# Joining attention and its output projection: the last head's last tiles transposed on TensorE, the first transposed load in two parts, the weight loads apart

## The chip, the cores and the metric

One core of a Trainium2 chip. The metric is the device time of one launch in microseconds (us). The engines are TensorE (PE, with its weight loads PEld), VectorE (DVE), ScalarE (ACT), GpSimd (POOL) and SyncE (SP), whose queue issues nearly all DMAs here. L559 is line 559 of the kernel before.

## The reference

A transformer block whose two halves are modulated by a condition c. D is 640, there are 2048 rows, 32 heads of 128, and 2048 cached keys and values for each head. Everything comes as bf16.

```python
mod = silu(c) @ w_mod                       # six rows: sa, ca, ga, sb, cb, gb
h = layernorm(x) * (1 + ca) + sa
q = (h @ wq) in 32 heads                    # wq: 640 x 4096
p = softmax(q @ k_cache^T / sqrt(128))      # 2048 x 2048 for each head
x = x + ga * ((p @ v_cache) @ wo)           # wo: 4096 x 640
h = layernorm(x) * (1 + cb) + sb
g = gelu(layernorm(h) @ w1)                 # w1: 640 x 640
hs = (four column groups of g shifted by +1, -1, +2, -2 rows) @ w2
x1 = h + hs
x = x + gb * (x1 + gelu(layernorm(x1) @ w3) @ w4)   # w3: 640 x 1728, w4: 1728 x 640
```

## The kernel before

**Planning.** `Prog` records every operation with the keys that it reads and writes, derives the semaphore waits from these, and emits the operations of each engine in the order in which they were recorded. So an engine's order is the order of the Python code, and a key that two operations share is a wait. SP's queue is such an order too: a DMA that waits holds those recorded after it.

**Score loop.** A tile is 128 rows of one head; there are NG = 512 tiles, 16 for each head, and step s of the loop begins tile s. PE multiplies queries and keys into `Sps` (L286), DVE scales with a minimum (L559, two halves), POOL joins the two minima (L569), ACT takes the exponential into `Pb`, one of eight rows of `ring` (L572). The probabilities have to be transposed for the product with the values: most tiles go in pairs through a DMA transpose on SP (`transpose`, L222), tiles 3 and 10 of each head through PE (`t_piece`, L253, into the banks `Oaug` and `QPp`), from which ACT (L262) or DVE (L264) copies them. `pv` (L299) multiplies with the values, 8 to 11 steps after the tile began; ACT copies each pair of results (L550), and POOL divides by the sums (`rcp` L440, `norm` L447) and writes four tiles at a time to `o_scratch` in DRAM (L454). Four tiles are a group, gr; head 31 has groups 124 to 127. The loop runs on past the last tile to step 523, for the products of the last eight tiles and their normalization.

**Output projection.** `load_ot(pr)` (L495) reads 256 rows of all 32 heads transposed from `o_scratch`: 64 blocks of 128x128, into `hTx` for even pr and into the place of `negS` for odd pr. It waits for the writes of all heads (`osd` keys). `load_xt` (L500) reads x again, in four parts, into rows of `ring` that tiles used before. The first `load_ot`, the four `load_xt` and the second `load_ot` follow each other on SP at step 512 and 513. Then i runs over 16 row tiles: `a_pe` (L631) multiplies with `wo`, 32 matmuls of 512 columns and 32 of 128, into one of two banks; `a_s1` and `a_s2` on DVE add, take statistics (L619, L621, with POOL's L612 and L614) and modulate; `nrm_of` (L662) writes a normed tile to one of three buffers, and `n_t` (L668) transposes it by DMA on SP. Statistics and the constant `mhalf` (L609) lie in the space of `On`, the buffer from which L454 writes.

**Second half.** `b_op` (L720; ACT evaluates gelu, L728) multiplies with w1, `c_op` (L740, DVE L744) with w2, `d_op` (L756, L760) with w3 and `e_op` (L772) with w4. The ten `b_op` of the first two column blocks come after the output projection; then each `c_op` is followed by one or two operations of a list of fillers, first `b_op`, then `d_op` and `e_op`. w3 and w4 go into the place of `wo` after the last product with it (L688, L689, L691), and all three loads write the one key `"wo"`.

Of the kernel before, what the change touches and what calls it, by code (L numbers as in the profile page):

```python
# [115 lines left out]
def bass_adaLN_cond__mha_block_cached__mixer_s_mlp__prompt_kernel(  # L116
# [6 lines left out]
    KT = D // 128  # L123
# [14 lines left out]
    with ExitStack() as es:  # L138
# [11 lines left out]
        if True:  # L150
            with ExitStack() as es1:
# [49 lines left out]
                G = Prog(nc, es1, "a")  # L201

                def load_k(h):
                    hb = h % 2
                    G.dma("sync", lambda e: e.dma_start_transpose(KTs[:, hb], A_k_cache[0, h]), ("k", hb), w=[("KT", hb)])
# [11 lines left out]
                assert RPB % 2 == 0 and RPT % 2 == 0 and NQT % 2 == 0  # L217
                is_pe = lambda g: g % NQT in PE_TILES

# [45 lines left out]

                by_dve = lambda g, r: r == 1 and g % NQT == PE_TILES[0]

# [64 lines left out]
                if H > 1:  # L332
                    load_wq(1)
                    load_k(1)
                G.dma("sync", lambda e: e.dma_start(wo[:], A_wo.rearrange("(h p) n -> p h n", p=128)), "wo", w=["wo"])

# [157 lines left out]
                def load_ot(pr):  # L494
                    G.dma("sync", lambda e: e.dma_start_transpose(OTj[pr % 2], o_scr[pr].rearrange("q h z d -> q (h z d)")),  # L495
                          ("ot", pr % 2), r=[("osd", pr // 2, hh) for hh in range(H)],
                          w=[("OT", pr % 2)] + ((HTK if pr == 0 else NEG) if pr < 2 else []))

# [7 lines left out]
                PVS, at = {}, []  # L506
                for g in range(NG):
# [5 lines left out]
                for g in range(NG):  # L513
                    NORMS.setdefault(at[g] + LAG, []).append(g)
                OT0 = max(NG, at[NG - NQT + 3] + LAG + 1)
                for s in range(at[-1] + LAG + 1):
                    h, j = divmod(s, NQT)
# [9 lines left out]
                    for half in range(2):  # L527
                        if s < NG:
                            qk(s, half)
                        for g_ in pvs:  # L530
                            if len(pvs) == 1:
                                pv(g_, half)
                            elif g_ == pvs[half]:
                                pv(g_, 0)
                                pv(g_, 1)
                        if s == 0 and half == 1:
                            q_head0(NQC - 1)
                        if h + 1 < H and 2 * j + half in QPIECE:
# [4 lines left out]
                        for r in range(2):  # L543
                            g = s - 3 - r
                            if 0 <= g < NG and is_pe(g):
                                t_piece(g, r, half)
                                if half == 1:
                                    evacs.append((t_evac, g, r))
                    for p in [g_ // 2 for g_ in pvs if g_ % 2 == 1]:
                        G.op("scalar", lambda a, p=p: a.copy(  # L550
                            Of[:, p % 4].rearrange("p z d -> p (z d)")[:, 0:259], PO[:, (p % 2) * 512:(p % 2) * 512 + 259]),
                            r=[("O", p % 2)], w=[("Of", p % 4)])
                    for fn, x, y in evacs:
# [14 lines left out]
                    if s < NG:  # L568
# [17 lines left out]
                    for g_ in NORMS.get(s, []):  # L586
# [11 lines left out]
                YB = [Sps[:, 0:1024], Sps[:, 1024:2048]]  # L598
                NB = [PTp[:, 0:1024], PTp[:, 1024:2048]]
# [3 lines left out]
                def ybank():  # L603
                    yn[0] += 1
                    return yn[0] % 2

                G.dma("sync", lambda e: e.dma_start(w1, B_w1.rearrange("(k p) n -> p k n", p=128)), "w1", w=["w1"] + KVK)
                G.dma("sync", lambda e: e.dma_start(w2, B_w2.rearrange("(k p) n -> p k n", p=128)), "w2", w=["w2"] + NEG)
                G.op("gpsimd", lambda g: g.memset(mhalf, -0.5), w=["mhalf"] + ONK)  # L609

# [12 lines left out]

                def a_pe(j):
                    b = ybank()
                    pr, z = divmod(j, 2)

                    def f(t):
                        for c0, cw in NC2:
                            for hh in range(H):  # L630
                                ins = t.matmul(YB[b][:, c0:c0 + cw], OTj[pr % 2][:, 2 * hh + z, :], wo[:, hh, c0:c0 + cw],  # L631
                                               start=(hh == 0), stop=(hh == H - 1))
                        return ins
                    G.op("tensor", f, r=[("OT", pr % 2), "wo"], w=[("S", b)])
                    return b

# [33 lines left out]

                for i in range(NQT + 1):
                    if i < NQT:
                        b = a_pe(i)
                        if i == NQT - 3:
                            for z in range(2):
                                G.op("gpsimd", lambda g, z=z: g.memset(us[:, :, z * SQ:z * SQ + 4], 0.0), w=[("usz", z), ("OT", 0)])  # L676
                        if i % 2 == 1 and (i + 3) // 2 < NQT // 2:
                            load_ot((i + 3) // 2)
                        a_s1(i, b)
                    if 1 <= i:  # L680
                        a_s2(i - 1)
                    if 2 <= i:
                        nrm_of(1, i - 2)
                        n_t(i - 2, i == 2)
                nrm_of(1, NQT - 1)
                n_t(NQT - 1, False)
                w3s = B_w3.rearrange("(k p) n -> p k n", p=128)
# [3 lines left out]
                G.dma("sync", lambda e: e.dma_start(w4[0:FL, NFT - 1, :], B_w4[(NFT - 1) * 128:FF, :]), "w4b", w=["w4b", "wo"])  # L691
                DEL = [1, -1, 2, -2]
# [22 lines left out]
                def b_op(cc, n):  # L715
# [14 lines left out]
                    G.op("scalar", ev, r=[("J", jb), ("usz", 0), ("usz", 1)], w=[("us", cc, n), ("OT", 0)])  # L730

                def c_op(j):
                    b = ybank()
# [29 lines left out]
                def e_op(j):  # L763
# [11 lines left out]
                    if j == NQT - 1:  # L775
                        for c0, cw in NC2:
                            G.op("tensor", lambda t, c0=c0, cw=cw: f(t, [(c0, cw)]), r=["w4", "w4b", ("gT", g)],
                                 w=[("S", b)] if c0 == 0 else [("S2", b)])
# [8 lines left out]
                        return  # L787
                    G.op("tensor", f, r=["w4", "w4b", ("gT", g)], w=[("S", b)])
                    G.op("vector", lambda v: v.tensor_add(out=tmp[:, u], in0=YB[b][:, 0:D], in1=xb[:, j]),  # L789
# [3 lines left out]
                    G.op("vector", lambda v: v.tensor_add(out=ob[:, u], in0=tmp[:, u], in1=xt[:, j]),  # L793
                         r=[("tmp", u), ("x1", j)], w=[("ob", u)] + (["wo"] if j < 2 else []))
# [56 lines left out]
```

## Time and profile before

| | us |
|---|---|
| runs shown: median of 3 (lowest, highest) | 1612.44 (1609.82, 1612.7) |
| the profiled execution | 1616.39 |
| its span | 1614.6 |
| PE busy in the span | 1483.7 (92%) |
| DVE busy | 1395.0 (86%) |
| ACT busy | 1268.3 (79%) |

The span is the time from the first to the last instruction that the profile holds; the execution's own time is 1.8 us longer. Matmuls overlap, so that PE counts as busy also where it is not at its peak. The core's mean granted TensorE clock is 0.993 of full speed. The chain of waits is followed back from the last instruction to what released each step; in the timeline, a bracket at a line's end tells how long the engine was idle before it and what ended that. "SPq" rows are the SP queue's own issue of a DMA, not the transfer.

### The profile page before, as it was taken

To read this page: it belongs to the slowest core of one execution; us is meant where nothing else is said; L and a number is where in the kernel's file an instruction comes from. 1 tells how busy PE (TensorE), PEld (TensorE's weight loads), DVE (VectorE), ACT (ScalarE), POOL (GpSimd) and SP (SyncE) were. 2 spreads that over 40 slices of the span, in tenths; PEclk is the share of its full clock that TensorE was granted. 3 is DMA by queue.
4 is the path that set the end of the run, shared out by engine and by line. 5 is a ranking of instruction groups with operands and counts; after the bars stand their busy time and mean duration, and the time that the engine had idled before them with its cause. 6 is when DMAs were issued, how large, how long until landed. Compare 5 with 4: busy or idle time off the path is not lost.

```text
span 1614.6 us, 34520 instructions
## 1 busy us (share of the span) xinstructions
PE 1483.7 (92%) x13820; PEld 954.8 (59%) x14071; DVE 1395.0 (86%) x2461; ACT 1268.3 (79%) x1113; POOL 627.2 (39%) x1396
## 2 busy tenths in 40 slices
PE   4799999999999999999999999998999699999999
PEld 3466666666666666666666666666666555544444
DVE  6999999999999999999999999998999446766424
ACT  4999999999999999999999999999999500033230
POOL 0144444444444444444444444444444513332100
PEclk9999999999999999999999999999999899999999
DMA  9999999999999999999999999999999998723100
GB/s 297 237 226 242 235 239 227 239 229 247 233 235 230 237 231 231 248 237 241 239 237 228 239 233 242 233 236 235 241 234 236 255 208 161 128 80 101 37 17 33
DMA packets 1189234, 338.85 MB, mean 210 GB/s; under 512 B 1169809, under 2 KB 1183057, under 8 KB 1189073
## 3 DMA queue, kind: packets, MB, share of 16 engines
q1 hardware_dynamic: 1182928, 319.83, 102.1%
q0 software_dynamic: 6144, 16.79, 3.1%
q8 instruction: 111, 1.82, 0.5%
q14 instruction: 51, 0.41, 0.1%
HBM read 43.48 MB, written 19.40 MB: 39 GB/s over the span
## 4 chain that ended last, share of the span: by engine, by line
DVE 25%; DMA 24%; ACT 23%; PE 18%; issue 9%; POOL 1%; SPq 0%; ACTq 0%; DVEq 0%; POOLq 0%
DVE negS L559 22%; DMA ring<-ring 21%; ACT ring L572 19%; PE Sps L631 7%; PE Sps L772 4%; PE Oaug L756 2%; PE QPp L756 2%; ACT ring L262 1%; ACT Of L550 1%; DMA wo<-in_B_w_dram 1%; ACT kv L244 1%; DMA ring<-in_A_x_dram 1%; DMA negS<-o_scratch 1%; DVE ring L364 1%; PE Sps L286 1%
## 5 line engine op out<-in xcount | busy, mean ns | idle before, releaser
L559 DVE TENSOR_SCALAR_CACHE_REDUCE negS<-Sps 128x1024 f32<-128x1024 f32 x1024 | 1180.1, 1225 | 38.8 <-ACT ring L572 18.8
L572 ACT ACTIVATE ring<-negS,small 128x2048 bf16<-128x2048 f32 x512 | 1007.7, 2017 | 39.6 <-DMA ring<-ring 33.7
L299 PEld LDWEIGHTS PTp<-kv,ring 128*128 128x128 bf16 x8192 | 560.1, 98 | 245.8 <-DMA ring<-ring 8.8
L286 PE MATMUL Sps<-kv 128*128 128x512 bf16 x1949 | 595.8, 383 | 76.1 <-DVE negS L559 54.9
L299 PE MATMUL PTp<-kv,ring 128*128 128x129 bf16 x8192 | 646.0, 221 | 6.9 <-DMA ring<-ring 6.8
L569 POOL TENSOR_SCALAR small<-small 128x1 f32<-128x1 f32 x512 | 146.5, 286 | 638.1 <-DVE negS L559 638.0
L286 PEld LDWEIGHTS Sps<-kv 128*128 128x128 bf16 x2048 | 126.8, 97 | 197.5 <-DVE negS L559 161.4
L447 POOL TENSOR_SCALAR On<-Of,small 128x128 bf16<-128x128 f32 x512 | 191.0, 374 | 13.0
L440 POOL TENSOR_TENSOR small<-Of,small 128x4 f32<-128x4 f32 x128 | 133.2, 1040 | 8.5 <-ACT Of L550 8.4
L454 POOL DMA_DIRECT2D o_scratch<-On x128 | 103.1, 806 | 40.8 <-POOL On L447 37.2
L237 PE MATMUL Oaug<-hTx,kv 128*128 128x512 bf16 x265 | 100.8, 385 | 12.7 <-ACT ring L262 7.7
L550 ACT COPY Of<-PTp 128x259 f32<-128x259 f32 x256 | 96.9, 379 | 11.0 <-PE PTp L299 11.0
L728 ACT ACT_TABLE_LOAD x1 | 1.3, 1283 | 129.8 <-POOL hTx L676 129.8
L237 PE MATMUL QPp<-hTx,kv 128*128 128x512 bf16 x259 | 96.7, 378 | 3.4 <-ACT hTx L391 2.7
L559 DVE DVE_READ_ACCUMULATOR negS<-Sps 128x1 f32 x1024 | 90.8, 89 | 0.0
L612 POOL TENSOR_SCALAR On<-On 128x1 f32<-128x1 f32 x48 | 24.3, 507 | 146.0 <-DVE On L621 146.0
L639 DVE TENSOR_TENSOR ring<-Sps,mod_bc 128x640 f32<-128x640 f32 x16 | 13.2, 825 | 74.1 <-PE Sps L631 74.1
L631 PE MATMUL Sps<-wo,hTx 128*128 128x128 bf16 (+1 forms) x504 | 71.1, 303 | 4.8 <-DMA hTx<-o_scratch 4.4
L631 PE MATMUL Sps<-wo,negS 128*128 128x128 bf16 (+1 forms) x504 | 69.1, 298 | 2.2 <-DMA negS<-o_scratch 1.8
L789 DVE TENSOR_TENSOR ring<-Sps,ring 128x640 f32<-128x640 f32 x15 | 12.4, 825 | 65.5 <-PE Sps L772 65.5
L262 ACT COPY ring<-Oaug 128x1024 bf16<-128x1024 bf16 x64 | 65.5, 1023 | 0.0
L631 PEld LDWEIGHTS Sps<-wo,hTx 128*128 128x128 bf16 x512 | 40.0, 99 | 36.1 <-DMA hTx<-o_scratch 4.3
(83 smaller groups left out, 986.7 us busy)
## 6 DMA issues: line engine op xcount, KB each, us to landing
kv<-in_A_v_cache_dram SPq DMA_DIRECT2D x32, 512.0 KB, 5.0
o_scratch<-On POOLq DMA_DIRECT2D x128, 128.0 KB, 5.4
ring<-in_A_x_dram SPq DMA_DIRECT2D x8, 640.0 KB, 4.9
kv<-in_A_wq_dram SPq DMA_DIRECT2D x32, 160.0 KB, 3.9
wo<-in_A_wo_dram SPq DMA_DIRECT2D x1, 5120.0 KB, 16.7
ring<-ring SPq DMA_TRANSPOSE x256, 7.2
ring<-in_w_mod_dram SPq DMA_DIRECT2D x1, 3200.0 KB, 14.2
out_dram<-wo SPq DMA_DIRECT2D x16, 160.0 KB, 1.8
```

The lines of the kernel that those rows point to most:

```text
L237: G.op("tensor", lambda t: t.matmul(JB[jb], wq[:, hb, q, :], hT[:, q, cc * 512:(cc + 1) * 512], start=(q == 0), stop=(q == KT - 1)), r=[(" ...
L262: G.op("scalar", lambda a: a.copy(dst, src), r=[("J", jb)], w=[("PT", g % RPT, r)])
L286: ins = t.matmul(Sps[:, col:col + 512], QT[:, hb, j * 128:(j + 1) * 128], KTs[:, hb, col:col + 512], start=True, stop=True)
L299: ins = t.matmul(ob[:, 0:129], PTs[:, b, kt, :], Vaug[:, hb, kt, 0:129], start=(kt == 0), stop=(kt == NKT - 1))
L440: G.op("gpsimd", lambda g: g.tensor_tensor(out=rl[:, 4 * b:4 * b + 4], in0=Of[:].rearrange("p a z d -> p (a z) d")[:, 4 * b:4 * b + 4, 128 ...
L447: G.op("gpsimd", lambda g: g.tensor_scalar(out=On[:, b, z, :], in0=Of[:, 2 * b + z // 2, z % 2, 0:128], scalar1=rl[:, 4 * b + z:4 * b + z ...
L454: G.dma("gpsimd", lambda e: e.dma_start(o_scr[jj // 2:jj // 2 + 2, :, hh].rearrange("a p z d -> p a (z d)"), On[:, b].rearrange("p (a z) d ...
L550: G.op("scalar", lambda a, p=p: a.copy(Of[:, p % 4].rearrange("p z d -> p (z d)")[:, 0:259], PO[:, (p % 2) * 512:(p % 2) * 512 + 259]), r= ...
L559: G.op("vector", lambda v, half=half, s=s, r8=r8: v.tensor_scalar(out=negS[:, s % 3, half * 1024:(half + 1) * 1024], in0=Sps[:, half * 102 ...
L569: G.op("gpsimd", lambda g, r8=r8: g.tensor_scalar(out=nm[:, r8:r8 + 1], in0=nm0[:, r8:r8 + 1], scalar1=nm1[:, r8:r8 + 1], scalar2=None, op ...
L572: G.op("scalar", lambda a, s=s, r8=r8: a.activation(Pb[:, s % RPB, :], negS[:, s % 3, :], ACT.Exp, bias=nm[:, r8:r8 + 1], scale=-1.0), r=[ ...
L631: ins = t.matmul(YB[b][:, c0:c0 + cw], OTj[pr % 2][:, 2 * hh + z, :], wo[:, hh, c0:c0 + cw], start=(hh == 0), stop=(hh == H - 1))
```

## The change

The last four tiles (508 to 511) are transposed by PE, with copies by DVE (five) and ACT (three); tile 506 now goes by DMA together with 507. The loop ends at step 511, and the value products of the last eight tiles are written out after it. The first `load_ot` is cut: 31 heads at step 504, head 31 (2 blocks) after the loop. Products 0 and 1 with `wo` are cut into pieces (`a_part`) that stand between the transposes and the value products. Group 124 is normalized at step 508 (before: at 510 and 511), group 126 last. The x loads and the second `load_ot` change their order, and w1 and w2 are recorded after the value products. The `b_op` of the first column block come before and after the last product with `wo`. The key `"wo"` becomes five keys, so that w3, w4 in two parts, and the rest of w4 each have their own; the w4 loads move behind `c_op` 4, 6 and 7. The core of the diff:

```diff
+                LAST_PE = NG - 4
+                LAST_DVE = ((LAST_PE, 0), (LAST_PE, 1), (LAST_PE + 1, 0), (LAST_PE + 1, 1), (LAST_PE + 3, 0))
+                is_pe = lambda g: g >= LAST_PE or (g % NQT in PE_TILES and (g < NG - NQT or g % NQT == PE_TILES[0]))
...
+                def load_ot0(h0, h1):
+                    G.dma("sync", lambda e: e.dma_start_transpose(
+                        OTj[0][:, 2 * h0:2 * h1, :], o_scr[0, :, h0:h1].rearrange("q h z d -> q (h z d)")),
+                        ("ot0", h0), r=[("osd", 0, hh) for hh in range(h0, h1)],
+                        w=[("OT", 0)] + HTK if h0 == 0 else [("OTB", 0)])
...
-                for s in range(at[-1] + LAG + 1):
+                for s in range(NG):
...
+                        if s == NG - 8:
+                            load_ot0(0, H - 1)
...
-                    if s == OT0:
-                        load_ot(0)
-                        for cc in range(NQC):
-                            load_xt(cc)
-                    if s == OT0 + 1:
-                        load_ot(1)
...
+                def a_part(j, h0, h1, parts):
+                    b = (j + 1) % 2
...
+                    G.op("tensor", f, r=[("OTB", 0) if pr == 0 and h0 == H - 1 else ("OT", pr % 2)] + WOK, w=[("S", b)])
...
+                def t_all(g, r):
+                    for q in range(2):
+                        t_piece(g, r, q)
+                    t_evac(g, r)
+                def pv2(g):
+                    for g_ in (g, g + 1):
+                        for half in range(2):
+                            pv(g_, half)
+                    of_copy(g // 2)
+                for g in (NG - 4, NG - 3):
+                    for r in range(2):
+                        t_all(g, r)
+                norm4(H * 4 - 3)
+                load_ot0(H - 1, H)
+                a_part(0, 0, H // 2, NC2[0:1])
+                for r in range(2):
+                    t_all(NG - 2, r)
+                a_part(0, H // 2, H - 1, NC2[0:1])
+                for r in range(2):
+                    t_all(NG - 1, r)
+                pv2(NG - 4)
+                a_part(0, 0, H - 1, NC2[1:2])
+                pv2(NG - 2)
+                norm4(H * 4 - 1)
+                load_xt(0)
+                load_ot(1)
+                for cc in range(1, NQC):
+                    load_xt(cc)
+                a_part(1, 0, H - 1, NC2)
+                for j in range(2):
+                    a_part(j, H - 1, H, NC2)
+                pv2(NG - 8)
+                pv2(NG - 6)
+                norm4(H * 4 - 2)
...
+                FIRST_B = {NQT - 2: (0, 1), NQT - 1: tuple(range(2, KT))}
...
                 for i in range(NQT + 1):
                     if i < NQT:
                         b = a_pe(i)
...
+                        for n in FIRST_B.get(i, ()):
+                            b_op(0, n)
                         a_s1(i, b)
...
-                G.dma("sync", lambda e: e.dma_start(w3, w3s), "w3", w=["w3", "wo"])
-                G.dma("sync", lambda e: e.dma_start(w4[:, 0:NFT - 1, :], B_w4[0:(NFT - 1) * 128, :].rearrange("(f p) n -> p f n", p=128)),
-                      "w4", w=["w4", "wo"])
-                G.dma("sync", lambda e: e.dma_start(w4[0:FL, NFT - 1, :], B_w4[(NFT - 1) * 128:FF, :]), "w4b", w=["w4b", "wo"])
+                G.dma("sync", lambda e: e.dma_start(w3, w3s), "w3", w=["w3", ("wo", 0)])
...
+                    if j in (4, 6, 7):
+                        load_w4((4, 6, 7).index(j))
...
-                for cc in range(2):
-                    for n in range(KT):
-                        b_op(cc, n)
+                for n in range(KT):
+                    b_op(1, n)
```

`norm4(gr)` is `rcp(gr)` and four `norm(gr, z)`. Products 0 and 1 in `a_pe` only name their bank now.

More of the change, by code (lines that the diff above doesn't have):

```diff
@@ L201, in bass_adaLN_cond__mha_block_cached__mixer_s_mlp__prompt_kernel @@
                 G = Prog(nc, es1, "a")
+                WOK = [("wo", i) for i in range(5)]
                 def load_k(h):
@@ L264, in t_evac @@
                         G.op("vector", lambda v: v.tensor_copy(dst, src), r=[("J", jb)], w=[("PT", g % RPT, r)])
-                by_dve = lambda g, r: r == 1 and g % NQT == PE_TILES[0]
+                by_dve = lambda g, r: (g, r) in LAST_DVE if g >= LAST_PE else r == 1 and g % NQT == PE_TILES[0]
+                TPIECE = {}
+                for g in range(LAST_PE):
+                    if is_pe(g):
+                        for r in range(2):
+                            TPIECE.setdefault(g + 3 + r, []).append((g, r))
                 taken = [u for j in PE_TILES for u in range(2 * (j + 3), 2 * (j + 5))]
@@ L512, in bass_adaLN_cond__mha_block_cached__mixer_s_mlp__prompt_kernel, with of_copy, norm4 @@
                 NORMS = {}
[L513 to L516 removed]
+                for g in range(NG - 12):
+                    gr = g // 4
+                    NORMS.setdefault(at[NG - NQT + 3] + 1 if gr == H * 4 - 4 else
+                                     max(at[gr * 4 + 3], at[g] + 2) if gr == H * 4 - 5 else at[g] + LAG, []).append(g)
+                assert at[-1] == NG - 1 and max(NORMS) < NG
+                def of_copy(p):
+                    G.op("scalar", lambda a: a.copy(
+                        Of[:, p % 4].rearrange("p z d -> p (z d)")[:, 0:259], PO[:, (p % 2) * 512:(p % 2) * 512 + 259]),
+                        r=[("O", p % 2)], w=[("Of", p % 4)])
+                def norm4(gr):
+                    rcp(gr)
+                    for z in range(4):
+                        norm(gr, z)
+                for s in range(NG):
                     h, j = divmod(s, NQT)
@@ L542, in bass_adaLN_cond__mha_block_cached__mixer_s_mlp__prompt_kernel @@
                                 evacs.append((q_evac, h + 1, cc))
[L543 to L548, printed above, removed]
+                        for g, r in TPIECE.get(s, []):
+                            t_piece(g, r, half)
+                            if half == 1:
+                                evacs.append((t_evac, g, r))
                     for p in [g_ // 2 for g_ in pvs if g_ % 2 == 1]:
-                        G.op("scalar", lambda a, p=p: a.copy(
-                            Of[:, p % 4].rearrange("p z d -> p (z d)")[:, 0:259], PO[:, (p % 2) * 512:(p % 2) * 512 + 259]),
-                            r=[("O", p % 2)], w=[("Of", p % 4)])
+                        of_copy(p)
                     for fn, x, y in evacs:
@@ new lines, in bass_adaLN_cond__mha_block_cached__mixer_s_mlp__prompt_kernel @@
+                G.dma("sync", lambda e: e.dma_start(w2, B_w2.rearrange("(k p) n -> p k n", p=128)), "w2", w=["w2"] + NEG)
+                G.op("gpsimd", lambda g: g.memset(mhalf, -0.5), w=["mhalf"] + ONK)
+                for i in range(NQT + 1):
+                    if i < NQT:
+                        b = a_pe(i)
+                        if i == NQT - 3:
+                            for z in range(2):
+                                G.op("gpsimd", lambda g, z=z: g.memset(us[:, :, z * SQ:z * SQ + 4], 0.0), w=[("usz", z), ("OT", 0)])
+                        if i % 2 == 1 and (i + 3) // 2 < NQT // 2:
+                            load_ot((i + 3) // 2)
+                        for n in FIRST_B.get(i, ()):
+                            b_op(0, n)
+                        a_s1(i, b)
+                    if 1 <= i:
+                        a_s2(i - 1)
+                    if 2 <= i:
+                        nrm_of(1, i - 2)
+                        n_t(i - 2, i == 2)
```

60 lines of the change are left out of this document (26 added, 34 removed).

## The prediction

> **What bounds the kernel now.** I read the busy time by stage first, with the stage limits taken from the chain of waits in order of time; then that chain; then the timeline of PE, POOL and the SP queue at the two seams that the change touches. Columns of the first view: start and end, length, then busy time and instructions of PE, PEld, DVE, ACT, POOL, then granted clock, DMA share, GB/s.
>
> ```profile
> 1270.00:1290.00 20.00, 9.40 (x125) 8.73 (x124) 0.01 (x1) 4.98 (x7) 11.54 (x22) 0.76 1.24 253
> 1290.00:1311.10 21.10, 19.27 (x126) 10.32 (x128) 4.42 (x8) 0.00 (x0) 0.85 (x3) 0.90 0.94 226
> 1311.10:1432.80 121.70, 120.97 (x882) 68.79 (x896) 81.25 (x151) 1.28 (x1) 40.52 (x58) 1.00 0.70 135
> 1432.80:1470.10 37.30, 31.69 (x166) 14.64 (x168) 24.51 (x48) 21.38 (x36) 9.88 (x18) 1.00 0.52 150
> 1470.10:1614.60 144.50, 139.54 (x803) 67.55 (x818) 62.85 (x100) 33.42 (x56) 12.90 (x22) 1.00 0.12 33
> ```
>
> The score loop ends near 1270. From 1311.1 to 1432.8 and from 1470.1 to the end PE is full, so what reaches those stretches earlier ends earlier by as much. Open time lies in the first two rows and in the fourth. The chain shows who holds them (start, length, what; lines are L numbers of the kernel):
>
> ```profile
> 1278.77 7.28 DMA o_scratch<-On
> 1286.05 1.33 SPq L495
> 1287.42 4.40 DMA ring<-in_A_x_dram
> ...
> 1298.02 12.84 DMA negS<-o_scratch
> 1310.86 0.27 issue
> 1311.13 8.64 PE Sps L631 x63
> ...
> 1454.39 8.48 DMA wo<-in_B_w_dram
> 1462.89 0.56 SPq L691
> 1463.49 2.78 DMA kv<-Of
> ```
>
> Until 1311 one SP queue leads: transposed loads and x loads one behind the other, then the second outputs' load (12.84). At 1454 to 1463 the w4 load stands ahead of the small transposes of the normed tiles. The timeline at those places:
>
> ```profile
> 1257.28 4.69 SPq L222 DMA_TRANSPOSE ring<-ring  x1
> 1262.02 4.26 SPq L222 DMA_TRANSPOSE ring<-ring  x1
> 1269.59 4.23 PE L299 MATMUL PTp<-kv,ring 128*128 128x129 bf16 x64 [0.74 <-DMA ring<-ring]
> 1275.66 2.04 PE L299 MATMUL PTp<-kv,ring 128*128 128x129 bf16 x32 [1.85 <-DMA ring<-ring]
> 1281.88 3.65 PE L299 MATMUL PTp<-kv,ring 128*128 128x129 bf16 x32 [4.17 <-DMA ring<-ring]
> 1288.87 0.78 POOL L454 DMA_DIRECT2D o_scratch<-On  x1 [0.29 <-POOL On L447]
> 1289.97 19.35 PE L631 MATMUL Sps<-wo,hTx 128*128 128x512 bf16 x126 [4.45 <-DMA hTx<-o_scratch]
> 1292.28 0.10 POOL L609 MEMSET On<- 128x1 f32 x1 [2.63 <-DMA o_scratch<-On]
> 1466.38 0.61 DVE L662 TENSOR_SCALAR Of<-ring,On 128x640 bf16<-128x640 f32 x1 [5.01 <-DMA kv<-Of]
> ```
>
> PE waits 1.85, 4.17 and 4.45 us for DMA transposes. After 1.85 us of idleness 32 value products took 2.04; after 4.17 they took 3.65, and the first wo product took 10.7 (1289.97 to the DVE's start at 1300.66) against 8.69 for each later one: the clock of 0.76 in the first table.
>
> **Part by part. 1. Outputs of 31 heads loaded early.** The load (62 blocks of 128x128) stands in SP's queue behind the transpose that starts at 1257.28, hence where the next pair starts now, 1262.02: the queue runs back to back here. Full loads of 64 blocks landed 11.5 to 14.9 us after issue, median 11.8 (line 495), and 62 blocks at the median give 11.4: PE may start its products at 1273.4 (1273.1 to 1276.5). Behind it come the pairs 504/505 and 506/507. A load holds the queue 8.0 (alone) to 11.6; I take 9.3 between busy neighbours, then 4.3 for each pair: issued at 1271.3 and 1275.6, landed 7.4 later, 1278.7 and 1283.0. The value products of these four tiles are put last on PE, so this delay lies under PE's other work. The x load must wait for the second pair (it overwrites its source), so it goes at 1283; the second outputs' load follows at 1283.7 and lands 12.84 later, at 1296.5. If all SP transposes cost 0.18 a block (11.56/64, the slowest row), it lands at about 1302.
>
> **2. What PE does from 1269.** Tiles 508 and 509 are transposed by PE with DVE copies of 0.69 (line 264), four of them after DVE's last minimum at 1270.0: done by about 1273, beside the wait for the load. POOL now normalizes group 124 at step 508 instead of 510/511: 1.04 + 1.42 + 0.8 ahead of the next minimum (L569), which may delay the exponentials of 509 to 511 by up to 2.6. Two ACT copies of 1.01 for tile 506 are gone at the same place, and PE wants tile 510 at 1277 only, so I cost it nothing; if that cover were gone it would be those 2.6. Then, in PE's order, from 1273.4: two wo products, 2 x 8.69 = 17.4; transposes of 510 and 511, 32 in eights (four take 0.39, so 8 take 0.44 to 0.78; I take 0.65) = 2.6; eight value products of 16, twice the 64 in 4.23 = 8.5. Together 28.5, with some joints of 0.05, 28.8: third product at 1302.2, not 1311.1. **Gain 8.9.** Value products at 0.94 each (as in the loop) and the shortest transposes would give 10.7.
>
> **3. The last normalization moves behind all that.** Group 126 is now the last written from buffer On, whose space the DVE statistics and the L609 memset take over; they wait until this write has landed. Now it is 6.75 from the end of the value products (1285.53) to the memset (1292.28), with a landing of 3.4. The changed one ends its products at 1302.1 amid w1, w2 and the third outputs' load, so I take the median landing 5.2 to 5.4: free at 1310.7. DVE has read product 0, but stands in its statistics; only after 0.9 + 0.2 + 0.84 does it free the bank of product 1, at 1312.6, where PE wants it at 1310.9. **Loss 1.6**; with landings of 3.3 to 7.3 (line 454), 0 to 3.8. DVE has 6.0 of work per 8.69 and catches up. w1 waits for the value products (1302), w2 and the third load (14.9 beside them) follow: landed near 1318, wanted at 1321, no cost.
>
> **4. First b products ahead.** Two of 1.08 go ahead of the last wo product (+2.2). Today 13.3 pass from its end to the first c product (1432.8 to 1446.1), led by ACT's evaluations; the third starts its ACT work 4.0 after that end, and would start it 1.06 after, so 10.4 remain. **Gain 0.8** (0 to 1.1).
>
> **5. w3 and w4 apart.** The w4 loads no longer wait on w3 in SP's queue. The wait of 5.01 on DVE and that of 3.8 on PE (1466.4 to 1470.1, by the chain's next piece) go; w3 would land about 22 after the last wo product, wanted 30 after. The w4 pieces need no wait of their own, and what they delay is wanted over ten us later. **Gain 3.8** (2.8 to 3.8). Thereafter PE's 144.5 stay.
>
> Sum: -8.9 + 1.6 - 0.8 - 3.8 = -11.9. The profiled execution took 1616.39 (span 1614.6 and 1.8 around it) and would take 1604.5. It lies 3.95 above the median of the runs, 1612.44 (1609.82 to 1612.7); the same sum from the median gives **1600.5**.
>
> **Rivals.** *The clock falls in the gap.* Between the loop's last value product (1268.9) and 1273.4 PE has only transposes and idle time, 4.5 us. If transposes keep it warm, the idle part is under 2 us, like the 1.85 that cost nothing; if not, it is like the 4.17 and 4.45, and costs the 2.0 of the first product (10.7 - 8.69): 1602.5. The trace has no transposes alone, so it leaves this open; 15%. The Trainium skill (TensorE: Matmul & The Clock Gate, Part 4: PE-mode transpose) says that transposes don't count as PE work for the clock; by that rule this rival holds, against the forecast.
>
> *The On write lands late*, only when the third load has cleared the DMA engines (1318): PE's fourth product starts at 1320 instead of 1312.6, and 1608 results. For: all share 16 engines. Against: line 454 landed in 7.3 at most amid full DMA. 9%.
>
> *Transposes stretch mildly*, so the second outputs' load binds: from 1302 on each us costs one. At 0.21 a block it lands near 1307: 1605.5. 8%.
>
> *Slower: the early load is late and PE's order holds everything behind it.* PE now puts 28.8 us of work, with the transposes of 510/511 and all eight value products, behind the first product's wait. Today half of that precedes it. Each us after 1273.4 is lost; from 1285.3 the whole gain is gone, and slower by 0.2% begins at 1288.5. If the load came when it comes now, 1289.97, the time would be 1617. For: SP's queue is full, and 31 heads' blocks share it with the pairs. Against: it would take 28 us where 14.9 is the worst row. The change would then not do what it says, the early load being no earlier. 8%, half of it beyond the 0.2%, some near zero.
>
> **How the numbers follow.** The forecast has 60%. About 0.2%, 3.2 us, is what a measurement of this kernel can tell from no change. The main rivals, clock, On and stretched loads, all stay faster. Faster 0.88, same 0.05, slower 0.07. The low end takes the shorter PE sum (1.8) and no On wait (1.6), and somewhat from the runs' own spread: 1596.5. The high end adds the late load (3.1) and cold clock (2.0) or the stretched loads: 1606.5.
>
> **What would show it.** L253 transposes after 1269 and wo products of 512 columns starting near 1273; a third product near 1302, with no wait on the negS load; a short PE wait before the fourth, behind DVE and the o_scratch write; c products at 3.5 us a step with no wait for a kv<-Of transpose, the first d product near 1458. Wrong if PE stands idle past 1277 for hTx, if wo products in the gap run at half rate for longer than 4 us, or if wo products wait on transposed loads after 1302.

## The result, and the profile after

| | before | changed |
|---|---|---|
| median of 20 runs each (us) | 1614.71 | 1607.49 |
| ratio, 95% interval | 1 | 0.9946 (0.9927 to 0.9965) |
| span of the profiled execution | 1614.6 | 1603.7 |

The change saves 0.54%, 8.7 us (5.7 to 11.8). The forecast was 11.9, so the direction is right and the size somewhat too large. As a time the forecast was 1600.5, reckoned from 1612.44; the kernel before now has 1614.71, so only the differences can be compared, and 8.7 lies within the 5.9 to 15.9 that the forecast's range amounts to. One execution of `dma_tiles` below, 6242.63 us, is left out of its ratio. The two spans differ by 10.9, but 4.2 of this lie in the score loop: its last minimum (L559 before, L583 now) ends at 1270.0 in one profile and at 1265.8 in the other, and tiles 16 to 480, whose instructions are the same, already took 1116.2 and 1111.5. All stage times below are therefore counted from the end of that minimum. So counted, the two programs end after 344.6 and 337.9.

Busy time by stage of the changed kernel (columns as in the prediction):

```profile
1265.80:1296.80 31.00, 27.81 (x305) 20.05 (x306) 4.83 (x7) 7.80 (x9) 6.78 (x13) 1.00 0.99 231
1296.80:1322.20 25.40, 19.97 (x131) 10.43 (x129) 12.24 (x24) 0.37 (x1) 9.26 (x17) 0.87 0.76 178
1322.20:1428.90 106.70, 106.70 (x783) 60.13 (x780) 71.51 (x133) 3.66 (x5) 35.31 (x51) 1.00 0.62 119
1428.90:1459.30 30.40, 29.38 (x161) 13.78 (x160) 23.74 (x47) 18.98 (x32) 10.13 (x18) 1.00 0.45 126
1459.30:1603.70 144.40, 141.14 (x821) 67.52 (x818) 63.66 (x100) 33.41 (x56) 12.88 (x22) 1.00 0.18 45
```

The first row reaches to the third wo product: 31.0 us where it was 41.1. PE is busy in 27.8 of them. The last two rows are as forecast. The second row is not: two products of 8.69 take 25.4 us, at a clock of 0.87. The chain of waits shows what stands there (the write of a group is L463 now, the memset L771, DVE's statistics L635, its read of a product's bank L659, the wo products L647):

```profile
1300.29 8.66 DMA o_scratch<-On
...
1309.20 0.90 DVE On L635 x2
...
1310.33 0.70 DVE ring L659
...
1311.07 1.04 PE Sps L647 x2
```

The last group's write takes 8.66 to land, and only then do DVE's statistics begin. And the timeline of PE:

```profile
1270.11 3.63 PE L647 MATMUL Sps<-wo,hTx 128*128 128x512 bf16 x16 [2.44 <-DMA hTx<-o_scratch]
1296.78 8.85 PE L647 MATMUL Sps<-wo,negS 128*128 128x512 bf16 x64
1311.07 11.30 PE L647 MATMUL Sps<-wo,negS 128*128 128x512 bf16 x64 [5.43 <-DVE ring L659]
1322.21 17.55 PE L647 MATMUL Sps<-wo,hTx 128*128 128x512 bf16 x128
```

The first 16 matmuls start 4.3 behind the minimum. The third product has no wait. The fourth waits 5.43 and then takes 11.1 (to 1322.21) instead of 8.69: after the pause PE runs at half rate for a while (granted clock 0.72 from 1311 to 1320).

### The profile page after: what moved, and what is told of

Same layout as the page of the kernel before. It is cut to its first block, busy times and chain, and to the rows that moved or that the text cites. A ratio compares the mean times of both kernels' runs of the same rounds, so it can differ in the third digit from the quotient of the medians.

```text
span 1603.7 us, 34871 instructions
## 1 busy us (share of the span) xinstructions
PE 1511.8 (94%) x14119; PEld 956.1 (60%) x14119; DVE 1397.1 (87%) x2466; ACT 1269.4 (79%) x1114; POOL 626.3 (39%) x1396
## 4 chain that ended last, share of the span: by engine, by line
ACT 32%; PE 21%; DMA 21%; DVE 17%; issue 8%; POOL 0%; ACTq 0%; DVEq 0%; POOLq 0%
ACT ring L596 26%; DMA ring<-ring 19%; DVE negS L583 15%; PE Sps L647 8%; PE Sps L845 4%; ACT ring L266 2%; ACT Of L535 2%; PE Oaug L829 2%; PE QPp L829 2%; ACT kv L248 1%; PE Sps L811 1%; PE PTp L308 1%; DVE ring L373 1%; PE Sps L295 1%; DMA hTx<-o_scratch 1%
## 5 line engine op out<-in xcount | busy, mean ns | idle before, releaser
L583 DVE TENSOR_SCALAR_CACHE_REDUCE negS<-Sps 128x1024 f32<-128x1024 f32 x1024 | 1179.2, 1221 | 35.8 <-PE Sps L295 17.7
L295 PE MATMUL Sps<-kv 128*128 128x512 bf16 x2048 | 618.3, 384 | 50.5 <-DVE negS L583 42.8
L241 PE MATMUL Oaug<-hTx,kv 128*128 128x512 bf16 x320 | 122.1, 386 | 11.2 <-ACT ring L266 8.3
L241 PE MATMUL QPp<-hTx,kv 128*128 128x512 bf16 x320 | 120.5, 381 | 2.6 <-ACT hTx L400 2.0
L463 POOL DMA_DIRECT2D o_scratch<-On x128 | 103.1, 806 | 40.8 <-POOL On L456 37.2
L583 DVE DVE_READ_ACCUMULATOR negS<-Sps 128x1 f32 x1024 | 85.9, 84 | 0.0
L647 PE MATMUL Sps<-wo,negS 128*128 128x128 bf16 (+1 forms) x512 | 73.0, 305 | 5.4 <-DVE ring L659 5.4
L647 PE MATMUL Sps<-wo,hTx 128*128 128x512 bf16 (+1 forms) x512 | 70.7, 299 | 2.4 <-DMA hTx<-o_scratch 2.4
L647 PEld LDWEIGHTS Sps<-wo,negS 128*128 128x128 bf16 x512 | 40.2, 99 | 37.8 <-DVE ring L659 5.6
L647 PEld LDWEIGHTS Sps<-wo,hTx 128*128 128x128 bf16 x512 | 39.4, 98 | 32.2 <-DMA hTx<-o_scratch 2.6
```

The lines of the kernel that those rows point to most:

```text
L241: G.op("tensor", lambda t: t.matmul(JB[jb], wq[:, hb, q, :], hT[:, q, cc * 512:(cc + 1) * 512], start=(q == 0), stop=(q == KT - 1)), r=[(" ...
L295: ins = t.matmul(Sps[:, col:col + 512], QT[:, hb, j * 128:(j + 1) * 128], KTs[:, hb, col:col + 512], start=True, stop=True)
L463: G.dma("gpsimd", lambda e: e.dma_start(o_scr[jj // 2:jj // 2 + 2, :, hh].rearrange("a p z d -> p a (z d)"), On[:, b].rearrange("p (a z) d ...
L583: G.op("vector", lambda v, half=half, s=s, r8=r8: v.tensor_scalar(out=negS[:, s % 3, half * 1024:(half + 1) * 1024], in0=Sps[:, half * 102 ...
```

## The experiments

Two theories of the missing microseconds: A, the write of group 126 lands late, DVE waits for its space, PE for DVE, and the clock falls in that pause; B, PE would be held at this place anyway, by a transposed load or by DVE's backlog. C and D ask why the write is late; E, F and G concern the clock in the earlier gap, between the loop's last value product and the first wo matmul. Line numbers shift by a few from kernel to kernel.

**The last value products earlier** (`pv_early`):

```diff
+                pv2(NG - 8)
+                pv2(NG - 6)
+                norm4(H * 4 - 2)
                 a_part(1, 0, H - 1, NC2)
...
-                pv2(NG - 8)
-                pv2(NG - 6)
-                norm4(H * 4 - 2)
```

> The value products of tiles 504 to 507 and the normalization of group 126 stand ahead of product 1 with wo instead of behind products 0 and 1; nothing else differs from the changed kernel. Theory A (the loss is the late write of group 126, for which DVE's first statistics wait, and the cold clock of the product behind that wait): PE's sum is the same, so the third product begins as far behind the loop's last minimum as now (about 31 us), but the write is issued some 8 us earlier, ahead of w1, w2 and the third outputs' load, and lands before DVE wants its space; the wait of 5.4 ahead of the fourth product and the 2.5 of its half-rate stretch go: 8 us less than the changed kernel, ratio to the kernel before about 0.989 to 0.991. Rival B (PE would be held there anyway, by a transposed load or by DVE's backlog): a wait of about 5 us stays ahead of the third, fourth or fifth product under another name, and the ratio stays near 0.9946.

Ratio to the kernel before 0.9907 (0.9874 to 0.9940). Timeline:

```profile
1293.51 0.09 POOL L771 MEMSET On<- 128x1 f32 x1 [1.91 <-DMA o_scratch<-On]
1297.18 17.55 PE L647 MATMUL Sps<-wo,negS 128*128 128x512 bf16 x128 [0.74 <-DVE ring L659]
```

The memset is through before the third product starts, the third and fourth products follow each other, and the wait of 5.43 and the slow product behind it are gone. The third product now waits 0.74 until DVE has read product 0's bank. The end comes at 332.6, 5.3 less than in the first profile of the changed kernel and not the 8 expected: the first 16 matmuls took 5.3 us, 1.7 more. As A says; B falls.

**The same order, another place for group 126** (`own_place`):

```diff
+                Onx = flat[:, 2560:3072].rearrange("p (z d) -> p z d", z=4)
...
+                    dst = Onx if own else On[:, b]
+                    ok = "Onx" if own else b
...
-                        norm(gr, z)
+                        norm(gr, z, gr == H * 4 - 2)
```

> Group 126 is normalized into 512 unused columns of ring and written from there, so that nobody on DVE waits for this write; its place in the order, and what it shares the DMA engines with, stay as in the changed kernel. Theory A: the write still lands 7 to 9 us after its issue, but DVE's first statistics begin 0.1 to 2 us after product 0's addition, the fourth product follows the third without a wait, and 8 us go (ratio 0.989 to 0.991). Rival B: DVE or PE still stand some 5 us at this place, ratio near 0.9946. If this kernel gains and the one with the early value products does not, it is the wait and not the order.

Ratio 0.9917 (0.9889 to 0.9945). The write still took 7.5 to land, and nobody waited for it:

```profile
1299.25 17.55 PE L651 MATMUL Sps<-wo,negS 128*128 128x512 bf16 x128
```

Third and fourth product again without a gap. So it is the shared space that makes the wait; the order alone, which stayed as it was, does not. The end is at 334.1; its first 16 matmuls were the slowest of all (6.31, below).

**w1 held until the write has landed** (`w1_behind`):

```diff
-"w1", w=["w1"] + KVK)
+"w1", r=[("osd", 2, H - 1)], w=["w1"] + KVK)
```

> SP holds the load of w1, and with it w2 and the third outputs' load, until the write of group 126 has landed; all else as in the changed kernel. Theory C (the write lands late, 8.7 us, because these 1.6 MB and the transposes share the DMA engines with it): the landing falls to 3.2 to 4.5 us, the wait ahead of the fourth product to under 1 us; the third outputs' load goes 6 us later, so that the fifth product waits for it 3 to 7 us, and little is gained in all. Rival D (a write from GpSimd's queue varies this much by itself): the landing stays at 7 to 9 us and the wait ahead of the fourth product at about 5.

```profile
1294.32 0.78 POOL L463 DMA_DIRECT2D o_scratch<-On  x1 [0.29 <-POOL On L456]
1296.65 0.09 POOL L771 MEMSET On<- 128x1 f32 x1 [1.55 <-DMA o_scratch<-On]
1310.93 4.27 PE L647 MATMUL Sps<-wo,hTx 128*128 128x512 bf16 x19 [2.56 <-DMA hTx<-o_scratch]
```

From issue to memset it takes 2.3 us instead of 8.7: the lateness comes from what SP sends beside it (C; D falls). The two weight loads and the third outputs' load were held together, so which of them it is stays open. The delayed third load costs the fifth product 2.56, less than the 3 to 7 expected. The end is at 334.7, 3.2 before that of the changed kernel; "little gained" was too dark.

**Transposes of 508 and 509 behind the first matmuls** (`t_late`):

```diff
-                for g in (NG - 4, NG - 3):
-                    for r in range(2):
-                        t_all(g, r)
                 norm4(H * 4 - 3)
                 load_ot0(H - 1, H)
                 a_part(0, 0, H // 2, NC2[0:1])
+                for g in (NG - 4, NG - 3):
+                    for r in range(2):
+                        t_all(g, r)
```

> PE's transposes of tiles 508 and 509 stand behind the first 16 wo matmuls instead of ahead of them, so PE does nothing at all from the loop's last value product to the landing of the first outputs (5 to 6 us). Theory E (in the changed kernel these transposes kept the clock at full rate: its first 16 matmuls took 3.63 us after 5.7 us with nothing but 32 transposes and 2.4 idle): now the 16 matmuls take 5 to 7 us, at half rate, and the third product begins 1.8 (the moved transposes) plus 1.5 to 2.5 later, 3.3 to 4.3 in all. Rival F (transposes do not count for the clock, and the gap was only too short to matter): the 16 matmuls take 3.5 to 3.7 as before and the third product begins 1.8 to 2 later.

The 16 matmuls took 5.04, the third product began at 35.7, 4.7 later than in the first profile of the changed kernel. That looked like E. But three kernels that keep the transposes in the gap showed the same slow stretch (5.31, 6.31, 5.18), so this run alone doesn't separate E from G, the theory of the next run that transposes do not keep the clock up.

**Matmuls for nothing in the gap** (`warm`, on top of `pv_early`):

```diff
+                def spin(n):
+                    def f(t):
+                        for _ in range(n):
+                            ins = t.matmul(YB[0][:, 0:512], ident[:], wo[:, 0, 0:512], start=True, stop=True)
+                        return ins
+                    G.op("tensor", f, r=["ident"] + WOK, w=[("S", 0)])
                 for g in (NG - 4, NG - 3):
                     for r in range(2):
                         t_all(g, r)
+                    spin(5 if g == NG - 4 else 9)
```

> The kernel with the early value products, plus 14 matmuls of 512 columns whose result nobody uses (5 between and 9 behind the transposes of tiles 508 and 509, into a bank that product 1 overwrites later), so that PE computes in the gap ahead of the first outputs. Theory G (PE's transposes do not keep the clock up; whether the gap of some 5.7 us costs anything depends on where it falls: the first 16 wo matmuls took 3.6 in one profile and 5.0 to 6.3 in four others): the 16 matmuls take 3.5 to 3.7 here, and the third product begins 1.7 us nearer to the loop's end than in the kernel with the early value products. Theory E (transposes keep it up; the slow stretches have another cause, such as a slow first read of the landed outputs): the 16 matmuls still take 5 or more. Time: 1 to 2 us under that kernel, which the runs may not resolve.

```profile
1264.78 3.63 PE L647 MATMUL Sps<-wo,hTx 128*128 128x512 bf16 x16 [0.30 <-DMA hTx<-o_scratch]
```

3.63 as G forecast, and the third product came at 31.7, 2.0 nearer than in `pv_early`. Ratio 0.9889 (0.9857 to 0.9921), which the runs can't tell from `pv_early`. So a slow first read of the landed outputs is out, and it is the clock. Against it the window of the 16 matmuls in `own_place`, where the figure behind the five engines is the granted clock:

```profile
1269.90:1276.10 6.20, 6.20 (x17) 2.29 (x18) 0.00 (x0) 0.00 (x0) 0.00 (x0) 0.56 1.34 263
```

But G says more than this run shows. Nine of the idle matmuls stand behind the last transposes and fill the time in which PE did nothing at all: 0.30 us of idleness are left ahead of the first wo matmul, against 2.44 to 3.92 in the six profiles with the transposes alone. That only this idleness costs, and the transposes do hold the clock, is a rival that no run tested by itself. The traces speak for it. The gap and the first matmuls, first two lines of `pv_early`, last two of `t_late`:

```profile
1262.10:1267.90 5.80, 2.27 (x37) 1.88 (x34) 3.89 (x8) 5.18 (x4) 2.63 (x6) 1.00 1.23 210
1267.90:1273.00 5.10, 5.07 (x16) 1.98 (x17) 0.00 (x0) 0.00 (x0) 0.92 (x2) 0.67 1.26 297
1259.30:1265.00 5.70, 0.00 (x0) 0.00 (x0) 1.16 (x4) 4.75 (x4) 2.75 (x6) 0.66 1.28 207
1265.00:1270.00 5.00, 4.94 (x18) 1.98 (x19) 0.00 (x0) 0.00 (x0) 0.81 (x1) 0.70 1.26 297
```

With the transposes in it the gap kept the full clock, which fell 0.9 us into the matmuls; with nothing in it the clock fell 1.8 us after the last value product. Over all profiles, where the clock fell in a pause with nothing in it, it did so 1.8 to 4.7 us after the last matmul (eleven cases). With the transposes in the pause it fell 4.0 to 6.5 us after the last value product, in four of six cases later than 4.7 (`ot_late`, below, is one of the six), and in the first profile of the changed kernel it did not fall there at all. So the transposes seem to hold the clock, and the idle time behind them to lose it. They seem to do so only in part: 2.55 us behind transposes cost the clock in `pv_early`, while plain waits of 2.56 in `w1_behind` and 2.99 in `dma_tiles`, ahead of the fifth product, did not.

**The last four tiles by DMA again** (`dma_tiles`; `t_all` of 508 to 511 left out, their value products last):

```diff
-is_pe = lambda g: g >= LAST_PE or (g % NQT in PE_TILES
+is_pe = lambda g: (g % NQT in PE_TILES
```

> The changed kernel with its first part undone: tiles 508 to 511 go through DMA transposes in the loop as before, and their value products stand last on PE, behind those of 504 to 507. Everything else stays. Theory H (with the outputs' products filling PE, these transposes are off the path; what they cost is SP's queue: two pairs of 4.3 us ahead of the second outputs' load): PE's sum is 1.8 shorter, the second outputs' load lands some 8.6 later, 32 to 33 us after the loop's last minimum, so the third product begins 1 to 2.5 us later than in the changed kernel (31 us) and waits for the load; time within 3 us of the changed kernel. Rival I (the transposes by TensorE carry most of the gain): PE waits for the last pair, the third product begins over 5 us later, and at least half of the gain over the kernel before is gone.

Ratio 0.9946 (0.9917 to 0.9974), just that of the changed kernel.

```profile
1295.88 17.33 PE L647 MATMUL Sps<-wo,negS 128*128 128x512 bf16 x126 [2.43 <-DMA negS<-o_scratch]
1316.20 4.05 PE L647 MATMUL Sps<-wo,hTx 128*128 128x512 bf16 x18 [2.99 <-DMA hTx<-o_scratch]
```

The third product waits for the second load and begins at 34.8, 3.8 later than in the first profile of the changed kernel (expected 1 to 2.5) and 0.7 later than in the second; about 2.4 is a cold start (products 0 and 1 took 19.8 instead of 17.4). In return SP reaches w1 only after the last group's write has landed, and the 5 us ahead of the fourth product are gone; the fifth waits 2.99. H holds: what the change is named after first brings no time by itself here. It frees SP, and the late write takes that back.

**w3 and w4 apart alone, in the kernel before** (`w34_only`; the change's lines for the `("wo", i)` keys and `load_w4`, nothing else).

> The kernel before with one part of the change alone: w3 and w4 under keys of their own, w4 loaded in three pieces behind c products 4, 6 and 7. By the prediction the waits of 5.0 on DVE and 3.8 on PE go, and the first d product begins 20.2 to 20.4 us after the first c product instead of 24.0: gain 3.8. Rival: the w4 pieces hold the small transposes instead, and 1 us or more of the wait stays.

First c product to first d product 20.1 instead of 24.0; neither wait is left. Gain 3.9, where 3.8 was forecast.

**First b products all behind the last wo product** (`b_after`):

```diff
-FIRST_B = {NQT - 2: (0, 1), NQT - 1: tuple(range(2, KT))}
+FIRST_B = {NQT - 1: tuple(range(KT))}
```

> The changed kernel with all five first b products behind the last wo product, as in the kernel before. By the prediction the first c product begins 13.3 us after the end of the last wo product instead of 10.3, and that end comes 2.2 earlier: 0.8 later in all. Rival (ACT's evaluations are hidden either way): no difference, or 2.2 gained.

It takes 13.3 from the end of the last wo product to the first c product, against 10.3; less the 2.2 that the two b products cost ahead, that is 0.8, as forecast.

**The first load behind the pairs** (`ot_late`):

```diff
-                        if s == NG - 8:
+                        if s == NG - 4:
                             load_ot0(0, H - 1)
```

> The changed kernel with the load of 31 heads recorded at step 508 instead of 504, so behind the DMA transposes of 504/505 and 506/507. By the prediction's slower rival, all of PE's work behind the first wo product moves with its wait: the load lands some 8.6 us later, the third product begins 8 to 11 us later than the 31.0 behind the loop's last minimum (39 to 42, with a cold start in it), and most of the gain over the kernel before is gone. Against that: if the value products and the second load had slack, less than half of the 8.6 would show at the third product.

```profile
1274.65 5.83 PE L647 MATMUL Sps<-wo,hTx 128*128 128x512 bf16 x15 [10.42 <-DMA hTx<-o_scratch]
```

PE starts at 12.3 instead of 4.3 and 5.3; the third product is at 41.4, as in the kernel before, and the end at 346.6, 2.0 behind it. Against the two profiles of the changed kernel the first matmul comes 8.0 and 7.0 us later and the end 8.7 and 7.3. So the slower rival's price is about right, one us of the end for each us of the first load's landing, and the place of this one DMA in SP's queue carries the gain of the first part.

**Both kernels once more** (`after_again`, `before_again`).

> The changed kernel once more, for what one profile of it may have had by chance. Theory A and C: the write of group 126 lands 7.5 to 9 us after its issue again, PE waits 5 to 6 ahead of the fourth product and then runs some 2.5 us longer at half rate. Theory G: the first 16 wo matmuls may take 3.6 as in the first profile or 5 to 6.3 as in four kernels that share this stretch; 5 or more would say that the first profile was the exception. The loop's last minimum falls anywhere between 1257 and 1270, as in the profiles so far.

```profile
1258.62 5.57 PE L647 MATMUL Sps<-wo,hTx 128*128 128x512 bf16 x15 [3.38 <-DMA hTx<-o_scratch]
1301.32 9.95 PE L647 MATMUL Sps<-wo,negS 128*128 128x512 bf16 x63 [5.24 <-DVE ring L659]
```

The wait is there again (5.24, landing 8.0), followed by a product of 10.0. The first matmuls are slow this time, so the first profile had been the exception. The end is at 339.3.

> The kernel before once more, for a second profile of its stages. From the exponential of tile 16 to that of tile 480 the profiles so far took 1116.2 and 1113.2 us with the loop of the kernel before, 1100.4 to 1111.5 in eleven profiles with the loop of the changed kernel, though the instructions of these 29 heads are the same. Theory J (this spread is chance): 1100 to 1112 here in most cases. Theory K (the loop itself runs a few us longer in this program): 1113 or more. Behind the loop, either way: third wo product 41 us after the loop's last minimum, first c product to first d product 24.0, last minimum to end 344 to 345.

Third product 41.1, first c to first d 24.4, end 344.9. From tile 16 to tile 480 it took 1106.1, inside the range of the others, as J says: single profiles of one loop differ by 10 us. That the loop runs a few us longer in this program (K) is not excluded: the three profiles with the loop of the kernel before average 1111.8, the eleven others 1107.9.

**Head 31's part of product 0 first** (`best`, on top of `warm`):

```diff
-                a_part(1, 0, H - 1, NC2)
-                for j in range(2):
-                    a_part(j, H - 1, H, NC2)
+                a_part(0, H - 1, H, NC2)
+                a_part(1, 0, H, NC2)
```

(A changed line of `a_part`, by which product 1, now in one piece, waits for both parts of the first load, is left out here.)

> The kernel with early value products and idle matmuls in the gap, and head 31's part of product 0 ahead of product 1 instead of behind it, so that DVE reads product 0's bank 8 us earlier. Expected from the profile of that kernel: the wait of 0.7 to 1.0 ahead of the third product goes, nothing else changes; ratio to the kernel before about 0.988, which the runs cannot tell from 0.989. Rival: the third product then waits for the second outputs' load, and the wait only changes its name.

Ratio 0.9877 (0.9842 to 0.9913), median 1589.29 against 1608.65 on that chip. The wait ahead of the third product goes (31.3), one of 0.6 for the third load comes at the fifth, and the end stays where `warm` has it. With the early value products and the matmuls in the gap the interval lies clear of that of the changed kernel (0.9927 to 0.9965) in both `warm` and `best`: they beat both kernels. This last step has no time of its own.

All in one table, us behind the loop's last minimum:

| kernel | first wo product | its first matmuls (16; 15 where starred) | third product | first c | first d | end |
|---|---|---|---|---|---|---|
| before | 20.0 | | 41.1 | 176.1 | 200.1 | 344.6 |
| before_again | 19.6 | | 41.1 | 176.1 | 200.5 | 344.9 |
| w34_only | 20.0 | | 41.4 | 176.4 | 196.5 | 340.9 |
| changed | 4.3 | 3.6 | 31.0 | 173.2 | 193.5 | 337.9 |
| after_again | 5.3 | 5.6* | 34.1 | 174.5 | 194.8 | 339.3 |
| b_after | 4.6 | 5.0* | 32.9 | 173.9 | 194.0 | 338.4 |
| t_late | 4.6 | 5.0 | 35.7 | 177.9 | 198.2 | 342.7 |
| ot_late | 12.3 | 5.8* | 41.4 | 181.8 | 202.1 | 346.6 |
| dma_tiles | 5.0 | | 34.8 | 171.7 | 192.0 | 336.4 |
| w1_behind | 4.8 | 5.2 | 33.1 | 169.9 | 190.2 | 334.7 |
| own_place | 5.8 | 6.3 | 35.2 | 169.3 | 189.6 | 334.1 |
| pv_early | 4.4 | 5.3 | 33.7 | 167.8 | 188.1 | 332.6 |
| warm | 4.1 | 3.6 | 31.7 | 165.8 | 186.1 | 330.6 |
| best | 4.4 | 3.6 | 31.3 | 165.8 | 186.1 | 330.5 |

## Why the prediction was right, and where not

The direction and the mechanism hold: the gain comes from PE starting the output products early and from the w4 load leaving SP's queue. By terms, forecast and the two profiles of the changed kernel, against the first profile of the kernel before:

| term | forecast | first | second |
|---|---|---|---|
| third product | -8.9 | -10.1 | -7.0 |
| group 126's write, with the slow product behind it | +1.6 | +8.0 | +6.5 |
| first b products | -0.8 | -0.9 | -1.1 |
| w3 and w4 apart | -3.8 | -3.7 | -3.7 |
| sum | -11.9 | -6.7 | -5.3 |

- **Part 1** was nearly right: PE could start 4.3 and 5.3 behind the minimum, not 3.4, and the second load was never waited for. `ot_late` shows that the position in SP's queue decides it.
- **Part 2** had PE's sum 2.1 too high: eight transposes take 0.45 and 32 value products 1.87, so 26.7 instead of 28.8, the low end that it gave. In the second profile a cold start takes the 2.1 back.
- **Part 3 is the term that was mis-sized.** The step was seen: the write from On lies last, and DVE's statistics wait for it. But it was put at 1.6 (1.7 by the prediction's own steps), and at 3.8 at most, and it measured 8.0 and 6.5. The landing was put at 5.2 to 5.4 and bounded by 7.3, from rows in which mostly SP's transposes ran beside such a write. Here two loads of 800 KB and a transposed load start within 3.3 us before it, and it took 8.7 and 8.0. The second omission is the after-effect: the clock falls in a pause of 5 us, which was priced for the earlier gap but not here; 2.5 and 1.3 us.
- **Part 4 and part 5** came out within 0.3, and `b_after` and `w34_only` show them alone.
- **The rival of the falling clock** had 15% and occurred in five of the six profiles with only the transposes in the gap; the first matmuls took 1.6 to 2.7 us more, near the 2.0 that it was given. With idle matmuls in the gap it did not occur in two of two. The prediction made it hang on whether transposes keep the clock up, with under 2 us of idleness if they do. But the transposes were done 1.9 behind the minimum, not 3, and the load came at 4.3 to 5.8, so that 2.44 to 3.92 were idle. The one fast profile had the 2.44; 2.55 was already slow. The Trainium skill says (TensorE: Matmul & The Clock Gate, Part 4: PE-mode transpose) that a transpose does not count as PE work in the same way. Taken as not counting at all, as the prediction took it, this gave the right outcome; but the traces shown with `warm` speak for counting in part. The same page of the Trainium skill (Part 1: The HAM clock gate) has the clock follow a window that runs free of the kernel; that the clock fell anywhere from 0.9 to 3.5 us behind the last transpose agrees with this, without proving it.
- **Slips in the working.** The prediction puts the slow first wo product down to the clock of 0.76; that row ends where this product begins, and over the product itself the clock was 0.81. The high end of the range lies 0.9 above the terms that it names (1600.5 + 3.1 + 2.0).
- **The rivals of the stretched and of the late first load** did not occur, and the late On write occurred in part.
- **Luck.** That the measured 8.7 lies within the forecast's range is not all of the prediction's making: of the gains by stage, 6.7 lies in the lower half of what the runs say, 5.7 to 11.8, and 5.3 just under it, as it lies under the forecast's 5.9 to 15.9. The other 2 to 3.4 us would have to lie ahead of the last minimum, where the forecast has no term. The loop there, whose length varies by 16 us between executions, keeps the runs from telling more.

## What to carry to other kernels

A buffer whose space gets a second use puts a wait between two steps that have nothing else in common; when the last writer moves to the end, look who takes over its space, and price the landing by what else will be in flight there, not by its median elsewhere. After making a gap shorter, look how long PE still stands idle at its end: a pause costs its length and then the slow stretch behind it, and a few matmuls for nothing can be cheaper. Parts that look like one idea have to be tried apart: here the position of one DMA in a queue carried the first gain, and the transposes that the change is named after none as long as the late write stood behind them.

## What the runs showed of the hardware that was not expected

The same 128 KB write from GpSimd's queue landed after 2.3 us with little beside it, 5.0 at the median amid SP's transposes, and 7.5 to 8.7 when two loads of 800 KB and a transposed load had just been issued. A stretch of 5.7 to 7.1 us in which PE transposes and then stands idle for 2.4 to 3.9 still had a mean clock of 0.82 to 1.00, and the matmuls behind it only 0.56 to 0.68, in five of six profiles. The recorded clock is full or half behind these pauses, and its half stretches last 3.41, 6.83 or 13.65 us. It can fall after work has begun again: in `pv_early` the first five wo matmuls start 0.22 us apart and those behind them 0.43. And the same loop of 464 steps took between 1100.4 and 1116.2 us in fourteen profiles, with no difference in its instructions.
